# Two table transfers moved later in a spectral filter stage, with its written order of steps re-sorted

## The chip, the core and the metric

The kernel runs on one core of a Trainium2 chip. The core has a matrix engine (TensorE, PE in the profile) that multiplies a 128-row weight tile by a streamed operand into PSUM, a vector engine (DVE), a scalar engine (ACT), a general-purpose engine (GpSimd, POOL) and a sync engine (SP) that mostly issues transfers. Each works through its own list of instructions in order, and they wait for each other through semaphores. 16 DMA engines carry the transfers, whoever issues them. The metric is the device time of one launch in microseconds: 997.96 us, the median of three runs of the kernel before (997.35 to 1001.58).

## What is computed

A block of four layers on x of shape 2048 x 640 (sequence by channels), each with a residual:

```python
x = x + A(layernorm(x)); x = x + B(layernorm(x)); x = x + A(layernorm(x)); x = x + B(layernorm(x))

def A(x):   # spectral filter: the filter stage of the title lies in here
    X = rfft2(x, axes=(-2, -1)) * (w_r + 1j * w_i)      # 2048 x 321 complex weights
    return irfft2(X, s=(2048, 640))

def B(x):   # token MLP with a GELU; w1 is 2048 x 1728, w2 is 1728 x 2048
    u = gelu(einsum("bsd,sf->bdf", x, w1) + b1)
    return transpose(einsum("bdf,fs->bds", u, w2) + b2)
```

## The kernel before

The Fourier transforms are done as matrix products with small tables, in float16 high and low parts so that a product of two split operands takes three matmuls. A layer A has a first part (`a0_...`: normalise, fold, transform along the long part of the sequence), the **filter stage** (`a1`) and a last part (`a2`: the inverse transform and the residual). `a1` runs twice in a launch, once per layer A; the first time (`first=True`) it also carries side work for later stages, hung in by the function `also`.

The filter stage takes 16 groups of frequencies, g = 0 to 15. Each group goes through steps that the code names by letters, the number behind them being the group:

- `d` (PE): products of the folded rows with the table tD, and with `stk`, a small stacked tile that SP brings for two groups at a time (three buffers; the load for groups n and n+1 waits until d of n-6 and n-5 have read theirs).
- `ph` (ACT) and `pl` (DVE): the high and low float16 parts of that result.
- `sA`, `sB` (PE): the two halves of the next small transform, with table tS2.
- `tb`, `ta` (DVE, `term`): the result times the filter weights `w[g]`. A weight tile of 321 KB is loaded by SP (`wload`); there are three buffers, and the load for group n is written down as soon as `ta` and `tb` of n-3 are.
- `sa`, `sb` (POOL, `suma` and `sumb`): the difference and sum that make the complex product. In the trace both write tile `ta`.
- `xh` (ACT), `xl` (POOL), `uh`, `ul` (ACT, `twice`): split into high and low parts, and a copied strip.
- `i` (PE, `is2mm`), `Yh` (ACT), `Yl` (DVE): first half of the inverse transform, and its split into the tile Y.

Four PSUM tiles (`slots`) hold what `d`, `sA`/`sB` and `i` write; the `@k` behind a step says which. A step may only write its slot when the readers of the last content are done: for instance `d10@1` writes the slot that `ta6` and `tb6` read.

The order of all steps is written out by hand in the string `STEPS`; the loop at the end of `a1` goes through it, and since everything in it is recorded with a mark that keeps program order (`self.pin`), each engine gets its own steps in the order of that string. The order between steps of different engines in the string has no meaning by itself, but three things hang on it: the place at which SP's loads of `w` and `stk` are written down (the code that follows `do(op)` in the loop), the place of the side work (`also`), and, in the kernel before, which ACT step after an `sA` is chosen for a dependency: `sB` of a group is made to follow one ACT step that itself follows `sA` (list `waiting`, function `acted`).

Two tables for `a2` are loaded during the filter stage from the POOL queue: tDi (966 KB) and the first of four parts of tIM (512 KB, tile `tIM0`). In the kernel before, both are issued behind `sb3`:

```python
if g == 3:
    with self.after(ins):
        nc.gpsimd.dma_start(self.tDi, A["tDi"])
        nc.gpsimd.dma_start(self.tIM0, A["tIM"][:, 0:4])
```

`a2` starts with products of Y and tDi (`id_mm`), and uses `tIM0` one step later (`is1_mm`). Nearly every instruction bears line 69 in the profile, that of the helper that records it (line 70 in the changed file, whose `STEPS` is one line longer), so tiles are the way to tell instructions apart. The loads keep their own lines: `w` L506, `stk` L494 and L496, tDi L654, tIM0 L655.

Of the kernel before, what the change touches and what calls it, by code (L numbers as in the profile page):

```python
# [24 lines left out]
FIRST = 2  # L25
WARM = 11
STEPS = '''
    d1@1 sA0@2 ph1 pl1 sB0 d2@0 sA1@1 ph2 tb0 d3@3 ph3 sB1 ta0 sa0 pl2 sb0 xh0 xl0 sA2@0 tb1 uh0 pl3 d4@2 ta1 sa1 sb1
    sB2 ph4 ta2 sA3@3 d5@1 ul0 pl4 tb2 sB3 sb2 ph5 pl5 sA4@2 xh1 sa2 d6@0 d7@1 ta3 ph6 tb3 sB4 pl6 tb4 xl1 uh1 ph7
    sA5@3 xh2 i0@0 sb3 sB5 pl7 sa3 ta4 ul1 Yh0 Yl0 tb5 sA6@1 xl2 xh3 ta5 sb4 d8@2 ph8 d9@0 sa4 xl3 xh4 sB6 uh3 ul3 sa5  # L30
    pl8 tb6 sA7@3 uh2 sb5 i1@2 ph9 sB7 Yh1 xl4 ta6 pl9 d10@1 xh5 sb6 xl5 sA8@0 sa6 Yl1 ul2 ta7 ph10 i3@2 tb7 sB8 Yh3
    pl10 sA9@3 i2@1 ta8 uh4 sa7 xh6 ul5 tb8 sB9 Yl3 d11@0 ul4 sb7 Yh2 Yl2 xh7 xl6 uh6 sb8 sa8 uh5 sA10@2 tb9 ph11 xl7
    ta9 pl11 d12@1 xh8 sB10 sa9 ph12 sb9 i4@3 Yh4 i5@0 ta10 tb10 pl12 xh9 Yh5 xl8 d13@2 Yl4 sb10 ph13 sA11@1 ul6 Yl5
    uh8 pl13 sA12@3 sB11 sa10 ul7 xl9 xh10 xl10 sB12 ta11 tb11 ta12 sA13@2 d14@0 ph14 ul8 sa11 i6@1 sb11 ul9 Yh6 uh7
    sB13 tb12 pl14 Yl6 d15@3 xh11 sa12 uh9 sA14@0 tb13 sb12 ph15 xl11 i7@1 sB14 ta13 pl15 uh10 i8@2 ul10 uh11 xh12
    sa13 Yh7 sb13 i9@3 ul11 xh13 uh13 tb14 ta14 xl12 Yl7 sa14 uh12 Yh9 sA15@0 Yh8 sb14 Yl9 xh14 xl13 i10@1 sB15 i11@3
    Yh10 ul13 Yl8 xl14 i13@2 Yh11 uh14 tb15a ta15a ul14 ul12 sb15a Yh13 tb15b sa15a ta15b Yl10 Yl11 i14@0 Yl13 xh15a
    sb15b i12@1 sa15b xl15a xh15b uh15 xl15b i15a@2 Yh14 Yh12 Yl14 Yl12 ul15 Yh15a i15b@3 Yh15b Yl15a Yl15b
'''
SEQ = [t + 7 * i for t in (6, 0, 1, 2, 3, 4, 5) for i in range(2)]  # L40
EPS = 1e-5
# [35 lines left out]
class Layers:  # L77
# [367 lines left out]
    def a1(self, first):  # L445
        nc, A = self.nc, self.A
# [90 lines left out]
        def xhi(g, c, x):  # L537

            return T.activation(xs[g % NX][0][:, :, c], x, AF.Copy)
# [6 lines left out]
        def twice(g, i):  # L546

            q = xs[g % NX][i]
            return T.activation(q[:, :, NL:], q[:, :, 257:320], AF.Copy)
# [61 lines left out]
        w = {g: wload(g) for g in range(3)}  # L611
        pp, ps2, pv = {}, {}, {}
        slots = [self.big() for _ in range(4)]
        dst, half, waiting = {}, {}, []
        tt = collections.defaultdict(dict)
        part = {"": every, "a": slice(0, 256), "b": slice(256, NL)}
        ltile = {"": slice(0, 3), "a": slice(0, 2), "b": slice(2, 3)}
# [7 lines left out]
            T.activation(b, a, AF.Copy, scale=sc)  # L625
            V.scalar_tensor_tensor(c, a, sc, b, op0=ALU.mult, op1=ALU.subtract)

        def acted(ins):

            for g in waiting:  # L630
                follow(ins, half[g])
                half[g] = ins
            waiting.clear()

        def do(op):

            name, g, c, dve, k = re.fullmatch(r"([a-zABY]+)(\d+)([ab]?)(!?)(?:@(\d))?", op).groups()
            g, W, ps = int(g), V if dve else G, slots[int(k or 0)]
            pair = lambda: (tt[g][0], tt[g][1])
            if name == "d":  # L640
                dst[g] = psplit(dstage(g, ps))
            elif name == "ph":
                acted(next(dst[g]))
            elif name == "pl":
                pp[g] = next(dst.pop(g))
            elif name in ("ta", "tb"):
                term(g, name == "tb", part[c])
            elif name == "sa":
                suma(pair(), part[c], W)
            elif name == "sb":  # L650
                ins = sumb(pair(), part[c], W)
                if g == 3:
                    with self.after(ins):
                        nc.gpsimd.dma_start(self.tDi, A["tDi"])  # L654
                        nc.gpsimd.dma_start(self.tIM0, A["tIM"][:, 0:4])  # L655
            elif name == "xh":
                acted(xhi(g, part[c], tt[g][0][:, :, part[c]]))
            elif name == "xl":
                xlo(g, part[c], tt[g][0][:, :, part[c]], W)
            elif name in ("uh", "ul"):  # L660
                acted(twice(g, name == "ul"))
            elif name == "sA":
                ps2[g] = ps
                half[g] = s2half(g, ps, pp[g], 0)[1]
                waiting.append(g)
            elif name == "sB":
                follow(s2half(g, ps2[g], pp.pop(g), 1)[0], half.pop(g))
            elif name == "i":
                pv[g, c] = ps
                for lt in range(3)[ltile[c]]:  # L670
                    is2mm(ps, g, lt)
            elif name == "Yh":
                acted(yhi(g, pv[g, c], ltile[c]))
            elif name == "Yl":
                ylo(g, pv[g, c], ltile[c])

# [37 lines left out]
        for op in STEPS.split():  # L714
            do(op)
            if first:
                also(op)
            ended.add(op.split("@")[0])
            if wn < NG and {f"ta{wn - 3}", f"tb{wn - 3}"} <= ended:
                w[wn] = wload(wn)  # L720
                wn += 1
            k = sn - NSTK * NC
            if sn < NG and (k < G0 or {f"d{k}", f"d{k + 1}"} <= ended):
                stack(sn)
                sn += NC
# [1298 lines left out]
```

## Time and profile before

| | |
|---|---|
| median of 3 runs | 997.96 us (997.35, 997.96, 1001.58) |
| the profiled execution: its time, its span | 999.61 us, 997.8 us |
| PE busy | 949.3 us (95%) |
| DVE busy | 774.9 us (78%) |
| ACT busy | 575.1 us (58%) |
| POOL busy | 302.1 us (30%) |
| first filter stage, first `d` step after the start to the first product with tDi | about 62.8 to 124.6 us |
| second filter stage, likewise | about 556.7 to 621.3 us |

The span is the time from the first to the last instruction of the profiled execution, and the execution's own time is 1.8 us longer. Busy shares are averages over stages that have different limits; the two filter stages are the places in which PE is not busy all the time, and they are read apart below. A timeline row gives start, duration, engine, line, operation, tiles written and read, how many instructions of that kind follow each other, and in brackets the idle time of the engine before it and who ended it.

### The profile page before, as it was taken

To read this page: it belongs to the slowest core of one execution; us is meant where nothing else is said; L and a number is where in the kernel's file an instruction comes from. 1 tells how busy PE (TensorE), PEld (TensorE's weight loads), DVE (VectorE), ACT (ScalarE), POOL (GpSimd) and SP (SyncE) were. 2 spreads that over 40 slices of the span, in tenths; PEclk is the share of its full clock that TensorE was granted. 3 is DMA by queue.
4 is the path that set the end of the run, shared out by engine and by line. 5 is a ranking of instruction groups with operands and counts; after the bars stand their busy time and mean duration, and the time that the engine had idled before them with its cause. 6 is when DMAs were issued, how large, how long until landed. Compare 5 with 4: busy or idle time off the path is not lost.

```text
span 997.8 us, 22816 instructions
## 1 busy us (share of the span) xinstructions
PE 949.3 (95%) x9126; PEld 703.5 (71%) x9126; DVE 774.9 (78%) x1488; ACT 575.1 (58%) x888; POOL 302.1 (30%) x512
## 2 busy tenths in 40 slices
PE   3879999999999999999999888999999999999998
PEld 2767777677776777777777666776777777677776
DVE  7979989988677884666666779789955666998885
ACT  4857859698656565555544457684644445454431
POOL 6939857322112102222222388583000000000000
PEclk9589999999999999999999999999999999999999
DMA  7856357657667655464431564574555447655411
GB/s 231 279 176 205 98 196 240 221 211 271 216 231 238 207 161 201 127 215 127 129 107 51 174 190 130 166 235 167 169 169 159 138 143 258 218 173 196 146 48 51
DMA packets 67454, 176.30 MB, mean 177 GB/s; under 512 B 8122, under 2 KB 15444, under 8 KB 67348
## 3 DMA queue, kind: packets, MB, share of 16 engines
q1 hardware_dynamic: 59380, 146.39, 46.2%
q0 software_dynamic: 7968, 28.46, 7.6%
q8 instruction: 71, 1.16, 0.5%
q14 instruction: 35, 0.29, 0.1%
HBM read 127.24 MB, written 47.58 MB: 175 GB/s over the span
## 4 chain that ended last, share of the span: by engine, by line
PE 61%; DVE 14%; issue 10%; DMA 5%; ACT 5%; POOL 4%; SPq 0%; POOLq 0%; DVEq 0%; ACTq 0%
PE ps L69 61%; DVE st L69 2%; DVE f L69 2%; DVE xt L69 1%; DMA w1S<-sp 1%; DVE s1l L69 1%; DMA raw<-w2z 1%; DVE hl L69 1%; DMA xt<-x 1%; POOL xt L69 1%; DVE Yl L69 1%; DVE wl L69 1%; DMA w<-w 1%; POOL w1A L935 1%; DVE S L69 1%
## 5 line engine op out<-in xcount | busy, mean ns | idle before, releaser
L69 PEld LDWEIGHTS <-wh 128*128 128x128 f16 x2602 | 251.5, 98 | 101.0 <-issue 2.4
L69 PEld LDWEIGHTS <-wl 128*128 128x128 f16 x1610 | 157.4, 98 | 63.2 <-DVE wl L69 1.3
L69 PE MATMUL ps<-ul,wh 128*128 128x320 f16 x448 | 133.0, 299 | 0.0
L69 PE MATMUL ps<-uh,wl 128*128 128x320 f16 x448 | 133.1, 299 | 0.0
L69 PE MATMUL ps<-uh,wh 128*128 128x320 f16 x416 | 124.3, 299 | 0.0
L69 PE MATMUL ps<-hl,wh 128*128 128x320 f16 x496 | 102.2, 299 | 0.8 <-DVE hl L69 0.8
L69 PEld LDWEIGHTS <-wo 128*128 128x128 f16 x756 | 73.9, 98 | 29.4 <-DVE wo L69 0.8
L69 DVE SCALAR_TENSOR_TENSOR wl<-raw,s,wh 128x896 f16<-128x896 f32 (+2 forms) x63 | 73.8, 1175 | 23.7 <-ACT wh L69 21.7
L69 POOL TENSOR_TENSOR r<-v,mh 128x1 f32<-128x1 f32 x64 | 37.3, 583 | 158.4 <-DVE nm L69 148.8
L69 ACT ACTIVATE junk<-raw 128x896 bf16<-128x896 f32 (+1 forms) x60 | 59.5, 992 | 32.0 <-DMA raw<-w 28.8
L69 PE MATMUL ps<-tDi,Yh 128*128 128x322 f16 x320 | 71.3, 300 | 0.4 <-ACT Yh L69 0.3
L69 ACT ACTIVATE wh<-raw,s 128x896 f16<-128x896 f32 (+2 forms) x66 | 66.5, 1032 | 5.5 <-DVE s L69 4.9
L69 DVE TENSOR_TENSOR f<-eo 128x256 f32<-128x256 f32 (+1 forms) x124 | 39.0, 367 | 37.8 <-POOL eo L69 37.0
L69 POOL TENSOR_TENSOR xt<-xt,ec 128x320 f32<-128x320 f32 x64 | 53.2, 853 | 32.7 <-DVE xt L69 32.6
L69 ACT ACTIVATE z<-xt,nb,r 128x640 f32<-128x640 f32 x31 | 28.5, 919 | 54.2 <-POOL z L69 43.1
L69 PE MATMUL ps<-u,wo 128*128 128x320 f16 x420 | 59.0, 299 | 0.5 <-DVE wo L69 0.5
L69 DVE BATCH_NORM_STATS2 st<-xt 128x6 f32<-128x320 f32 x126 | 55.2, 479 | 5.3 <-DMA xt<-x 4.7
L69 PE MATMUL ps<-hha,wh 128*128 128x320 f16 x288 | 58.1, 299 | 0.9 <-DVE wh L69 0.9
L69 PE MATMUL ps<-tM,f 128*128 128x128 f32 x160 | 37.6, 402 | 21.7 <-DVE f L69 21.6
L69 POOL TENSOR_TENSOR eo<-z 128x320 f32<-128x320 f32 x60 | 52.2, 891 | 17.2 <-ACT z L69 15.2
L69 PE MATMUL ps<-tDi,Yl 128*128 128x322 f16 x192 | 55.7, 299 | 1.4 <-DVE Yl L69 1.4
L69 PE MATMUL ps<-hha,wl 128*128 128x320 f16 x256 | 53.4, 299 | 1.0 <-DVE wl L69 1.0
(254 smaller groups left out, 2335.5 us busy)
## 6 DMA issues: line engine op xcount, KB each, us to landing
xt<-x SPq DMA_DIRECT2D x79, 320.0 KB
raw<-w SPq DMA_DIRECT2D x32, 512.0 KB
w<-w SPq DMA_DIRECT2D x48, 321.0 KB
x<-xt SPq DMA_DIRECT2D x47, 320.0 KB
raw<-w SPq DMA_DIRECT2D x32, 448.0 KB
raw<-w2z SPq DMA_DIRECT2D x32, 448.0 KB
w1S<-sp POOLq DMA_DIRECT2D x20, 512.0 KB, 3.9
out<-xt SPq DMA_DIRECT2D x15, 320.0 KB
```

The lines of the kernel that those rows point to most:

```text
L69: i = f(*a, **k)
L935: (self.nc.sync if k else self.nc.gpsimd).dma_start(st[:, i], w[i][:, c * q:c * q + q])
```

## The change

It does four things.

1. The steps in `STEPS` are written in another order. On each single engine the order of the steps stays what it was; only how the four lists are interleaved in the string differs.
2. The choice of the ACT step that an `sB` follows is no longer derived from the place in the string but written down with the step (`ph1&0` means: this step is the one between `sA0` and `sB0`). The pairs are those of before.
3. tDi is loaded in two halves (its high and its low part), behind `sb7` and `sb9`, and the first part of tIM behind `sb11`; before, both were loaded whole behind `sb3`.
4. Since loads and side work are written down where the string puts them, a few of these move: in both filter stages SP's load of `w` for group 3 comes ahead of the `stk` load for groups 8 and 9 instead of behind it, and in the first filter stage five side instructions on ACT stand one place earlier or later.

```diff
 STEPS = '''
-    d1@1 sA0@2 ph1 pl1 sB0 d2@0 sA1@1 ph2 tb0 d3@3 ph3 sB1 ta0 sa0 pl2 sb0 xh0 xl0 sA2@0 tb1 uh0 pl3 d4@2 ta1 sa1 sb1
+    d1@1 sA0@2 ph1&0 pl1 sB0 d2@0 tb0 ta0 sA1@1 d3@3 ph2&1 sa0 sb0 pl2 sB1 ph3 sA2@0 tb1 xh0 d4@2 uh0&2 pl3 xl0 ta1
...
-        def acted(ins):
+        def acted(ins, gs):
 
-            for g in waiting:
+            for g in map(int, gs.split(",") if gs else ()):
                 follow(ins, half[g])
                 half[g] = ins
-            waiting.clear()
...
-                if g == 3:
+                if g in (7, 9, 11):
                     with self.after(ins):
-                        nc.gpsimd.dma_start(self.tDi, A["tDi"])
-                        nc.gpsimd.dma_start(self.tIM0, A["tIM"][:, 0:4])
+                        if g < 11:
+                            nc.gpsimd.dma_start(self.tDi[:, g // 9], A["tDi"][:, g // 9])
+                        else:
+                            nc.gpsimd.dma_start(self.tIM0, A["tIM"][:, 0:4])
```

**POOL in the second filter stage**, around the loads of tDi and tIM; before (`xl` ... is the step `xl1`, the row behind it `sb3`, then the two loads, `sa3`, `xl2`):

```order
L69 TENSOR_TENSOR xl_1063_8366<-ta_8699,xh_1063_8365 128x2x321
L69 TENSOR_TENSOR ta_8879<-tb_8884,ta_8879 128x321
L654 DMA tDi_8359<-tDi 128x3864
L655 DMA tIM_8358<-tIM 128x1024
L69 TENSOR_TENSOR ta_8879<-ta_8879,tb_8884 128x321
L69 TENSOR_TENSOR xl_1063_8368<-ta_8720,xh_1063_8367 128x2x321
```

and in the changed kernel (`sa7`, `sb7`, the first half, `xl6`, `sb8`, `sa8`, `xl7`, `sa9`, `sb9`, the second half, `xl8`):

```order
L70 TENSOR_TENSOR ta_9216<-ta_9216,tb_9259 128x321
L70 TENSOR_TENSOR ta_9216<-tb_9259,ta_9216 128x321
L655 DMA tDi_8360<-tDi 128x1932
L70 TENSOR_TENSOR xl_1063_8367<-ta_9149,xh_1063_8366 128x2x321
L70 TENSOR_TENSOR ta_9291<-tb_9333,ta_9291 128x321
L70 TENSOR_TENSOR ta_9291<-ta_9291,tb_9333 128x321
L70 TENSOR_TENSOR xl_1063_8369<-ta_9216,xh_1063_8368 128x2x321
L70 TENSOR_TENSOR ta_9444<-ta_9444,tb_9405 128x321
L70 TENSOR_TENSOR ta_9444<-tb_9405,ta_9444 128x321
L655 DMA tDi_8360<-tDi 128x1932
L70 TENSOR_TENSOR xl_1063_8371<-ta_9291,xh_1063_8370 128x2x321
```

The two issues behind `sb3` are gone; a half-size issue stands between `sb7` and `xl6`, another between `sb9` and `xl8`, and the load of tIM likewise between `sb11` and `sa12`. POOL's other instructions keep their order.

**SP in the second filter stage**, around the load of `w` for group 3 (`w_8644` before, `w_8577` now); the `stk` tile for groups 8 and 9 is `stk_8621` before and `stk_8623` now, that for groups 6 and 7 `stk_8519`. Before:

```order
L494 DMA stk_8621<-rest_12_1063_8376 32x4x256
L496 DMA stk_8621<-rest_12_1063_8376 1x256
L506 DMA w_8644<-w 128x642
L506 DMA w_8701<-w 128x642
L895 DMA raw_10415<-w 128x1024
```

and now:

```order
L495 DMA stk_8519<-rest_12_1063_8377 32x4x256
L497 DMA stk_8519<-rest_12_1063_8377 1x256
L507 DMA w_8577<-w 128x642
L495 DMA stk_8623<-rest_12_1063_8376 32x4x256
L497 DMA stk_8623<-rest_12_1063_8376 1x256
```

The load of `w` for group 3 has moved ahead of the five issues for `stk` of groups 8 and 9; behind them the load for group 4 and that of a weight tile of layer B (`raw`) follow as before.

**ACT in the first filter stage**, around the side work on `raw` (the sums of squares, `junk`). Before (`ul1`, `Yh0`, `junk`, `xh3`, `ph8`, `xh4`, `uh3`, `ul3`, `junk`, `uh2`):

```order
L69 ACTIVATE xl_219_881<-xl_219_881 128x2x63
L69 ACTIVATE Yh_871<-ps_908 128x2x96x4
L69 ACTIVATE junk,sq_1527<-raw_1418 128x1024
L69 ACTIVATE xh_219_884<-ta_1411 128x2x321
L69 ACTIVATE ph_1580<-ps_910 128x2x321
L69 ACTIVATE xh_219_886<-ta_1515 128x2x321
L69 ACTIVATE xh_219_884<-xh_219_884 128x2x63
L69 ACTIVATE xl_219_885<-xl_219_885 128x2x63
L69 ACTIVATE junk,sq_1527<-raw_1420 128x1024
L69 ACTIVATE xh_219_882<-xh_219_882 128x2x63
```

and now:

```order
L70 ACTIVATE xl_219_881<-xl_219_881 128x2x63
L70 ACTIVATE Yh_871<-ps_908 128x2x96x4
L70 ACTIVATE xh_219_884<-ta_1372 128x2x321
L70 ACTIVATE junk,sq_1572<-raw_1419 128x1024
L70 ACTIVATE ph_1613<-ps_910 128x2x321
L70 ACTIVATE xh_219_886<-ta_1515 128x2x321
L70 ACTIVATE xh_219_884<-xh_219_884 128x2x63
L70 ACTIVATE junk,sq_1572<-raw_1421 128x1024
L70 ACTIVATE xl_219_885<-xl_219_885 128x2x63
L70 ACTIVATE xh_219_882<-xh_219_882 128x2x63
```

The first `junk` now stands behind `xh3`, the second ahead of `ul3`; three more side instructions (one on b1, two splits of a weight tile) change places with a neighbour in the same way. DVE's list and PE's are the same in both kernels.

36 lines of the change are left out of this document (18 added, 18 removed).

## The prediction

> **What bounds the kernel now.** I read the stages of the trace first, then the chain of work that ended last inside the second filter stage, then the timelines there. The stretches are the first filter stage, what lies between, the second filter stage, and the rest; behind the stretch and its length come busy times of PE, weight loads, DVE, ACT and POOL with counts, the granted clock, the DMA share and GB/s:
>
> ```profile
> 62.80:124.60 61.80, 56.08 (x1484) 45.01 (x1480) 55.13 (x101) 45.17 (x93) 48.77 (x62) 0.99 0.51 152
> 124.60:556.70 432.10, 426.46 (x3278) 311.22 (x3280) 322.12 (x733) 264.04 (x372) 115.92 (x218) 1.00 0.56 184
> 556.70:621.30 64.60, 57.16 (x1487) 46.57 (x1484) 52.34 (x82) 40.65 (x83) 49.01 (x62) 0.96 0.55 167
> 621.30:997.80 376.50, 369.68 (x2696) 267.12 (x2696) 292.48 (x429) 182.65 (x245) 43.58 (x70) 1.00 0.50 163
> ```
>
> Between and behind the filter stages PE is busy 98 to 99% of the time, so a microsecond gained in a filter stage reaches the end. The second one is the longer by 2.8 us although it carries no side work, and its clock is lower. The chain of waits there (start, length, what) says why:
>
> ```profile
> 576.11 0.80 DVE ta L69
> 576.92 7.30 DMA w<-w
> 584.34 0.20 DVE tb L69
> 585.14 0.89 DVE ta L69
> 586.07 14.04 PE ps L69 x344
> ```
>
> One transfer of filter weights takes 7.30 us, and nothing else in the stage has a piece of that kind. The timeline around it:
>
> ```profile
> 574.76 0.57 POOL L654 DMA_DIRECT2D tDi<-tDi  x1
> 575.32 0.56 POOL L655 DMA_DIRECT2D tIM<-tIM  x1
> 576.92 3.00 SPq L506 DMA_DIRECT2D w<-w  x3
> 579.48 0.82 DVE L69 SCALAR_TENSOR_TENSOR pl<-ps,ph 128x642 f16<-128x642 f32 x1
> 584.34 0.89 DVE L69 SCALAR_TENSOR_TENSOR tb<-ps,sx,w 128x642 f32<-128x642 f32 x1 [4.04 <-DMA w<-w]
> 586.07 0.48 PE L69 MATMUL ps<-tD,s1h 128*64 128x160 f16 x4 [4.01 <-DVE ta L69]
> 590.37 0.83 DVE L69 SCALAR_TENSOR_TENSOR pl<-ps,ph 128x642 f16<-128x642 f32 x1 [1.11 <-ACT ph L69]
> ```
>
> By its place in DVE's list the late `tb` is `tb6`, and the load is that of `w` for group 6. It is issued 2.2 us behind tDi and 1.6 us behind tIM. DVE stands for 4.04 us; behind it stand `ta6`, and PE with `d10`, whose PSUM slot `ta6` reads: 4.01 us. Four more stretches (columns as above) show the transfers at their limit during that wait, what PE's clock does behind it, and who is busy from then on:
>
> ```profile
> 576.50:584.50 8.00, 5.38 (x144) 4.42 (x137) 3.90 (x7) 4.98 (x10) 7.06 (x8) 1.00 1.01 339
> 586.05:589.30 3.25, 3.23 (x44) 2.43 (x43) 3.21 (x5) 0.00 (x0) 2.83 (x3) 0.50 0.37 106
> 591.20:611.70 20.50, 20.35 (x564) 16.12 (x556) 20.49 (x32) 16.49 (x38) 18.59 (x20) 1.00 0.52 159
> 84.00:89.00 5.00, 4.32 (x118) 3.46 (x113) 4.51 (x8) 4.08 (x11) 5.00 (x7) 1.00 1.07 363
> ```
>
> In the 8 us around the wait the DMA engines are full and move 2.7 MB (339 GB/s). Of this, tDi and tIM are 1.5 MB (966 and 512 KB). After the wait PE runs at a granted clock of 0.50 for 3.25 us. From 591 to 612 PE and DVE are both busy without a gap and POOL nearly so. The last row is from the first stage: there the engines are full too, but no DVE row waits for `w`.
>
> **The change, part by part.**
>
> *The stall at `tb6` (second stage).* With tDi and tIM gone from here, 1.5 of the 2.7 MB are gone. What is left for `w` of group 6 to wait for is its own queue. The nearest row for its landing is the load of group 3, issued with the load of group 4 and the 512 KB `raw` behind it:
>
> ```profile
> 568.26 0.99 SPq L506 DMA_DIRECT2D w<-w  x2
> 572.17 0.89 DVE L69 SCALAR_TENSOR_TENSOR ta<-ps,sx,w 128x642 f32<-128x642 f32 x1 [0.21 <-DMA w<-w]
> ```
>
> It took 3.91 us from issue to use. `tb6` can start when DVE is through with `pl8`, at 584.34 - 4.04 = 580.30, 3.38 us after the issue. So the load comes 0.53 us late if it takes as long as that row, and not at all if it is quicker. The issue itself should come sooner: the load of group 3 moves ahead of five `stk` issues on SP (they wait for `d3`, the load only for `ta0` and `tb0`), so 0.33 MB leave the crowded stretch from 568 on, about 1 us at the rate above. That also removes the 0.21 us of `ta3`. I take 0.2 us late, with 0 and 0.53 as bounds.
>
> Gone with the wait is the slow clock: 3.25 us at 0.50 instead of 1.00 is 1.6 us for PE, so PE could gain 4.01 + 1.6 = 5.6 us. DVE follows directly: 4.04 and the 1.11 us that `pl10` waited for the slow `d10`, 5.15 us. DVE then has 20.49 us of work in 20.50 us, so it is the narrower one, and I take its figure: 5.15 - 0.2 = 4.95 us.
>
> *The new places of the three issues (second stage).* Each issue held POOL for 0.56 to 0.57 us; a half-size one is not in the trace, and I take the same. Behind `sb3` POOL gets 1.13 us back. The one behind `sb7` falls into a wait:
>
> ```profile
> 592.61 1.42 POOL L69 TENSOR_TENSOR xl<-ta,xh 128x642 f16<-128x642 f32 x1 [1.75 <-ACT xh L69]
> 597.48 0.74 POOL L69 TENSOR_TENSOR ta<-tb,ta 128x321 f32<-128x321 f32 x1
> ```
>
> That row is `xl6`, which has 1.75 us to spare. The second half stands behind `sb9` (the row at 597.48), tIM behind `sb11`, both where POOL works without a break: 1.13 us later for `xl8`, `sb12` and what follows. Queued behind them are `ul` and `xh` on ACT and then `i` on PE. If all of it reaches PE, 1.13 us are lost; POOL's idle share of that stretch (20.50 - 18.59 = 1.91 us) would absorb it. Nearer to that row, I take 0.4 us.
>
> *The moved transfers.* They now meet later loads of `w`. Those have more room than group 6 had:
>
> ```profile
> 594.63 0.87 DVE L69 SCALAR_TENSOR_TENSOR tb<-ps,sx,w 128x642 f32<-128x642 f32 x1
> 595.42 0.88 DVE L69 SCALAR_TENSOR_TENSOR ta<-ps,sx,w 128x642 f32<-128x642 f32 x1
> 603.45 0.87 DVE L69 SCALAR_TENSOR_TENSOR ta<-ps,sx,w 128x642 f32<-128x642 f32 x1
> 621.27 0.45 PE L69 MATMUL ps<-tDi,Yh 128*128 128x322 f16 x2
> ```
>
> The load for group 12 may go when `tb9` and `ta9` are done (596.30) and is first used by `ta12` at 603.45: 7.15 us, the tightest of groups 9 to 13. A half of tDi is 0.49 MB, 1.5 us at 339 GB/s; 3.91 + 1.5 = 5.4 us still fits. The cover is 1.7 us; without it each load costs what its lateness is. tDi is first used at 621.27, 24 us behind `sb9`; whole, it landed in 5.9 us:
>
> ```profile
> tIM<-tIM POOLq DMA_DIRECT2D x2, 512.0 KB, 5.5
> tDi<-tDi POOLq DMA_DIRECT2D x1, 966.0 KB, 5.9
> ```
>
> So both tables are in time, and the moved transfers cost nothing there.
>
> *The first filter stage.* No `w` is late here, so only POOL's and ACT's lists matter.
>
> ```profile
> 82.54 0.78 POOL L69 TENSOR_TENSOR ta<-ta,tb 128x321 f32<-128x321 f32 x1
> 87.70 1.04 ACT L69 ACTIVATE junk<-raw 128x1024 bf16<-128x1024 f32 x1
> 88.74 0.29 ACT L69 ACTIVATE xh<-xh 128x126 f16<-128x126 f16 x1
> 89.08 0.33 PE L69 MATMUL ps<-ph,tS 64*64 64x321 f16 x4 [0.76 <-ACT xh L69]
> ```
>
> `sB7` waits 0.76 us for `uh2` on ACT, and that came late behind a `junk` of 1.04 us and POOL's chain. `sa3` (82.54) moves up by 1.13 us, and the `junk` no longer waits for `ul3`. So 0 to 0.76 us are won; later the same issues as above cost 0 to 1.13 us in a stretch where POOL has less idle time to share out (POOL is 5.00 of 5.00 us busy from 84 to 89), of which the 1.13 us won at `sb3` pay a part. I take the middle of 0 and 0.76, a gain of 0.4 us. SP's swap makes the `stk` load of groups 8 and 9, issued from 71.66 on, wait for `w` of group 3, which goes as soon as `ta0` and `tb0` are done, here at 72.10; its first reader `d8` starts at 83.54, so that is hidden:
>
> ```profile
> 71.22 0.88 DVE L69 SCALAR_TENSOR_TENSOR ta<-ps,sx,w 128x642 f32<-128x642 f32 x1
> 71.66 0.30 SPq L494 DMA_DIRECT2D stk<-rest  x1
> 83.54 0.33 PE L69 MATMUL ps<-tD,s1h 128*64 128x160 f16 x4
> ```
>
> *Explicit pairs* for `sB` cost nothing: they are those of before.
>
> **The sum.** 4.95 - 0.4 + 0.4 = 4.95 us. Against the profiled execution's 999.61 us (span 997.8 and 1.8 us around it) that gives 994.7 us. That execution was 1.65 us above the median of the runs, 997.96 us, and I take the gain off the median: **993.0 us**.
>
> **The rivals.**
>
> *The queues share evenly.* If SP's and POOL's transfers took turns, group 6 would have had half of the engines all along, and taking POOL's away would only halve the data part of its 7.30 us. With a fixed part between 0 and the 3.91 us of the row above, it would then land after 3.65 to 5.6 us: 0.3 to 2.2 us late. For it speaks that three `w` loads and one `stk` load stood in SP's queue as well. Against it, tDi and tIM landed by 580.8 (574.76 + 5.9, 575.32 + 5.5) and group 6 not before 584.2, so POOL's seem to have had most. At 2.2 us late the gain is 5.15 - 2.2 - 0.4 + 0.4 = 2.95 us: 995.0 us. The Trainium skill has this rule ("DMA: Bandwidth & Descriptors", section "SWDGE vs HWDGE vs iDMA"): each DMA engine goes round-robin between its internal queues, and those fed by GpSimd and those fed by the sync engine are different ones. The landing times just named fit it only if a turn of tDi is much longer than a turn of `w`.
>
> *POOL becomes the bound.* The three issues (1.7 us) stand where POOL is 91 to 100% busy. Before, it could wait for the late DVE in between, here at `sb6`:
>
> ```profile
> 586.10 0.75 POOL L69 TENSOR_TENSOR ta<-tb,ta 128x321 f32<-128x321 f32 x1 [2.54 <-DVE ta L69]
> ```
>
> If DVE and PE could come 5 us sooner but POOL could not, what remains is POOL's own waits, the 2.54 us here and the 1.75 us at `xl6`, less 1.7: 2.6 us. With the first stage losing 1.1 us the time is 996.5 us. Against it: the 1.13 us at `sb3` come back.
>
> *Slower.* A moved transfer meets a load of `w` and DVE stops as it did at `tb6`, in a stretch where it has no spare time. It decides from 7.15 us of landing time on; a wait of 4 us needs 11.2 us. Each such wait is worth 4.0 + 1.6 us with the clock behind it: 997.96 - 4.95 + 5.6 = 998.6 us if it comes in one stage, 1004.2 us in both. A DMA share of 0.52 in that stretch, where the wait at `tb6` had 1.01, speaks against it.
>
> *It doesn't do what it says.* The order on each engine is unchanged, so the sorting alone is worth nothing; if `w` of group 6 were late for SP's own traffic alone, the time stays at 997 to 999 us. The full engines with 1.5 of 2.7 MB from POOL speak against that.
>
> **How the numbers follow.** Forecast 0.74, with a range of its own of 991 to 995; even sharing 0.09; POOL as the bound 0.06; slower 0.07; nothing 0.04. About what a measurement of this kernel can tell from no change is 0.5%, 5.0 us, so the bound for faster is 992.97 us, and the forecast stands on it. Its best end is PE's 5.6 us with 0.76 us from the first stage and nothing lost to POOL, 991.6 us; its worst 0.53 us late, 1.13 us lost to POOL and no gain in the first stage, 994.5 us; half a microsecond on each side is for the runs' own spread. I put half of the forecast, 0.37, on faster; the other half with sharing, POOL and nothing, 0.56, on the same; 0.07 on slower. The range for 8 in 10 is 990.6 to 997.5: it takes in sharing and POOL, and leaves out slower, most of nothing and a little below.
>
> **What would show it.** In the changed profile the second filter stage should have no PE idle piece of several microseconds in front of `d10`, `tb6` should wait for `w` at most 0.5 us, and the granted clock of that stage should be near 1.00; its length should fall from 64.6 to about 60. In the first stage the wait of `sB7` should shrink. If PE instead waits in the second half for `xl`, `ul` or `xh`, the POOL term was too small; if `tb6` still waits 1 us or more, the sharing rival is right; a wait of 1 us or more at `tb9` to `tb13` with `w` as the releaser would make the forecast wrong on the slower side.

## The result, and the profile after

The changed kernel takes **991.58 us** (median of 5 runs, 990.41 to 991.67) against 997.96 us of the kernel before (5 runs, 997.35 to 1001.58): a ratio of 0.9926, with a 95% interval of 0.9911 to 0.9941. On a second chip, later, it took 991.93 us (5 runs, 990.50 to 992.84) beside 997.63 us: 0.9947 (0.9934 to 0.9960). The forecast was 993.0 us and put most of its weight on no measurable change; what came is a gain of about 6 us, beyond the 0.5% that the prediction had set as the bound (on the second chip just beyond it: 0.53%, with an interval that begins at 0.40%).

The same four stretches of the profile after, cut as far ahead of the first `sA0` of a stage, and as near the first product with tDi, as before (stretch, length, busy time of PE, weight loads, DVE, ACT and POOL, granted clock, DMA share, GB/s):

```profile
61.15:121.95 60.80, 55.67 (x1482) 44.47 (x1478) 54.92 (x101) 45.98 (x95) 49.58 (x63) 1.00 0.55 160
121.95:552.95 431.00, 425.42 (x3260) 310.00 (x3260) 320.95 (x732) 264.34 (x373) 116.01 (x218) 1.00 0.55 184
552.95:613.40 60.45, 55.87 (x1501) 45.23 (x1502) 53.60 (x84) 40.99 (x83) 49.34 (x63) 1.00 0.61 184
613.40:989.80 376.40, 369.66 (x2696) 267.10 (x2696) 292.55 (x428) 182.58 (x245) 43.58 (x70) 1.00 0.50 163
```

The profiled execution took 991.63 us, with a span of 989.8 us: 8.0 us less than the profiled one before. Of these, 4.15 us are in the second filter stage (64.60 to 60.45) and 1.0 us in the first (61.80 to 60.80). 1.1 us lie between the stages and 1.65 us ahead of the first one, where the change moves nothing. Those are dealt with under the first experiment.

DVE's rows in the second stage after the change, at the place of the late load (in brackets the idle time before a row), with SP's loads of `w` and POOL's three issues:

```profile
570.20 0.35 SPq L507 DMA_DIRECT2D w<-w  x1
574.25 3.16 SPq L507 DMA_DIRECT2D w<-w  x3
575.38 0.89 DVE L70 SCALAR_TENSOR_TENSOR tb<-ps,sx,w 128x642 f32<-128x642 f32 x1 [0.41 <-DMA w<-w]
577.72 0.89 DVE L70 SCALAR_TENSOR_TENSOR tb<-ps,sx,w 128x642 f32<-128x642 f32 x1
584.19 0.57 POOL L655 DMA_DIRECT2D tDi<-tDi  x1
590.34 0.56 POOL L655 DMA_DIRECT2D tDi<-tDi  x1
597.84 0.54 POOL L657 DMA_DIRECT2D tIM<-tIM  x1
```

`tb6` (577.72) starts without a wait; its load of `w`, issued at 574.25, was there within 3.47 us, where it took 7.30 us before. What is left is 0.41 us at `tb5`, the step one group earlier. Half a table costs POOL 0.57 and 0.56 us, as much as a whole one. The stretch of 8 us around the place, and the 20.5 us from the first issue on:

```profile
572.10:580.10 8.00, 7.75 (x212) 6.39 (x208) 7.59 (x12) 6.31 (x13) 7.79 (x9) 1.00 0.67 192
584.10:604.60 20.50, 20.08 (x551) 15.73 (x545) 19.73 (x31) 16.27 (x37) 20.45 (x24) 1.00 0.73 234
```

The DMA share in the crowded 8 us has gone from 1.01 to 0.67, and PE's busy time there from 5.38 to 7.75 us. The bytes are now in the later stretch (0.73 instead of about 0.5), where PE is still busy 20.08 of 20.50 us and POOL has no idle time left.

In the first stage the waits of PE, from `d4` to the first product with tDi, were before (us in total, times, longest):

```profile
PE ps L69 <- DVE Yl L69: 2.1, 4, 0.8
PE ps L69 <- ACT xh L69: 0.8, 1, 0.8
PE ps L69 <- ACT xl L69: 0.4, 1, 0.4
PE ps L69 <- DVE ta L69: 0.3, 1, 0.3
PE ps L69 <- ACT Yh L69: 0.3, 1, 0.3
```

and after:

```profile
PE ps L70 <- DVE Yl L70: 2.3, 4, 1.0
PE ps L70 <- DVE ta L70: 0.4, 1, 0.4
PE ps L70 <- ACT Yh L70: 0.2, 1, 0.2
```

Two waits for ACT are gone, that of `sB7` (`xh`, 0.8) and one for `xl` (0.4) that the prediction did not speak of; those for `Yl` and `ta` are longer by 0.2 and 0.1 us.

### The profile page after: what moved, and what is told of

It is laid out like the page before. It is cut to its first block, busy times and chain, and to the rows that moved or that the text cites. A ratio compares the mean times of both kernels' runs of the same rounds, so it can differ in the third digit from the quotient of the medians.

```text
span 989.8 us, 22823 instructions
## 1 busy us (share of the span) xinstructions
PE 946.2 (96%) x9126; PEld 700.2 (71%) x9126; DVE 774.9 (78%) x1488; ACT 575.6 (58%) x888; POOL 302.9 (31%) x514
## 4 chain that ended last, share of the span: by engine, by line
PE 62%; DVE 10%; issue 10%; DMA 7%; POOL 5%; ACT 5%; SPq 0%; POOLq 0%; ACTq 0%; DVEq 0%
PE ps L70 62%; DMA xt<-x 2%; DMA w<-w 2%; DVE xt L70 1%; DVE hl L70 1%; DVE st L70 1%; POOL xt L70 1%; DMA raw<-w2z 1%; POOL w1A L936 1%; DMA w1S<-sp 1%; DVE f L70 1%; DVE s1l L70 1%; DVE S L70 1%; DVE wl L70 1%; POOL eo L70 1%
```

## The experiments

The theory: the 7.30 us of the one load of `w`, behind tDi and tIM, are nearly all of it in the second stage; POOL's 1.13 us and the moved side steps make the 1 us in the first. The rivals: that the re-sorted list and SP's swap do part of it; that POOL's new issue places take part of it away; that what delays the load is not the bytes.

| run | median, runs | kernel before beside it | ratio (95%) | wait of `tb6` in the trace |
|---|---|---|---|---|
| loads alone | 991.41, 8 | 997.54 | 0.9944 (0.9925-0.9963) | none (`tb5` 0.31) |
| order alone | 997.21, 12 | 997.54 | 1.0000 (0.9984-1.0016) | 3.00 |
| loads, second stage only | 992.77, 12 | 997.54 | 0.9956 (0.9939-0.9973) | none |
| before, again | 998.87, 12 | 997.54 | 1.0016 (1.0000-1.0033) | 4.39 |
| changed, again | 991.93, 5 | 997.63 | 0.9947 (0.9934-0.9960) | 0.39 |
| tIM back | 992.55, 11 | 997.63 | 0.9948 (0.9930-0.9966) | 1.27 |
| six issues | 994.00, 12 | 997.63 | 0.9969 (0.9958-0.9980) | 2.40 (see there) |
| raw later | 991.75, 7 | 997.63 | 0.9947 (0.9929-0.9965) | none |
| tDi back on POOL | 994.84, 12 | 997.61 | 0.9966 (0.9946-0.9986) | 3.28 |
| tDi on SP, ahead of `w` | 996.11, 12 | 997.61 | 0.9976 (0.9954-0.9998) | 1.84 |
| tDi on SP, last | 993.33, 12 | 997.61 | 0.9955 (0.9936-0.9973) | none |
| both of the last ideas | 993.58, 12 | 997.61 | 0.9955 (0.9935-0.9975) | none |

Times are in us. Rows with the same figure for the kernel before ran on one chip.

### The kernel before, again

No edit.

> The kernel before, unchanged, for a second trace of it and for the scatter of one kernel against itself: 0 within 0.5 us. The wait of about 4 us at tb6 and the granted clock of 0.5 behind it should be there again. Open is the granted clock at the start of the second filter stage (0.50 at 556 to 558 us in the trace of before, 1.00 in that of the change): if it belongs to the kernel it is low here too, if it is chance it is not, and then up to 1.4 us of the 8.0 us between the two profiled spans is not the change's.

The kernel against itself gives 1.0016, and its 12 runs lie between 996.1 and 1001.8 us: single executions of one kernel differ by several microseconds. The trace shows one source. The granted clock (next to last but one number of a row) at the start of the second stage, in the first trace of before and in this one:

```profile
555.60:559.00 3.40, 3.40 (x56) 3.40 (x58) 1.23 (x2) 0.24 (x1) 1.71 (x3) 0.54 0.94 302
```

```profile
560.20:563.70 3.50, 3.50 (x56) 2.69 (x53) 0.92 (x2) 0.71 (x1) 1.45 (x2) 0.53 0.32 88
```

PE ran at half clock for about 3.4 us both times, the first time ahead of `sA0`, the second time behind `d2`. The first trace of before also had such a stretch at the start of the first stage, twice as long; the second one had none there:

```profile
57.00:63.80 6.80, 5.62 (x56) 4.98 (x58) 2.83 (x6) 4.14 (x10) 1.46 (x3) 0.50 0.78 263
```

In the other traces they came, or not, around the starts of either filter stage, with the loads at the old places and at the new. Two examples with loads moved: the loads alone, at the start of the first stage, and tDi on SP ahead of `w` (see below), at the start of the second, again of the double length:

```profile
67.80:71.20 3.40, 3.40 (x53) 2.59 (x50) 2.77 (x6) 0.71 (x1) 1.28 (x2) 0.50 0.30 80
```

```profile
562.60:569.40 6.80, 6.59 (x94) 5.03 (x94) 2.08 (x4) 2.04 (x3) 1.45 (x2) 0.52 0.46 131
```

So they are not the change's, and 3.4 us at half speed are worth up to 1.7 us where PE has work throughout. The trace of the change happened to have none from the first stage on. The stretches from 57 and from 555.6 us in the trace of before both lie ahead of an `sA0`; they are large enough for the 2.75 us outside the filter stages, and the reason why the spans of two single traces must not be subtracted. The Trainium skill ("TensorE: Matmul & The Clock Gate", section "Part 1: The HAM clock gate (the 'warmup' mystery)") says that the gate watches windows of about 3.4 us that run freely, without regard to the program. The lengths of these stretches (3.4 and 6.8 us) and their coming and going agree with that.

To compare the stages without those stretches, I take each from `d4`, behind the start, to the first product with tDi. Before, and after, `d4` and the product in the first stage:

```profile
73.42 0.33 PE L69 MATMUL ps<-tD,s1h 128*64 128x160 f16 x4
124.65 0.31 PE L69 MATMUL ps<-tDi,Yh 128*128 128x322 f16 x1 [0.27 <-ACT Yh L69]
```

```profile
71.77 0.33 PE L70 MATMUL ps<-tD,s1h 128*64 128x160 f16 x4
122.01 0.45 PE L70 MATMUL ps<-tDi,Yh 128*128 128x322 f16 x2 [0.22 <-ACT Yh L70]
```

and in the second stage, before (the product is at 621.27, in the prediction) and after:

```profile
566.81 0.33 PE L69 MATMUL ps<-tD,s1h 128*64 128x160 f16 x4
```

```profile
564.07 0.33 PE L70 MATMUL ps<-tD,s1h 128*64 128x160 f16 x4
613.34 0.45 PE L70 MATMUL ps<-tDi,Yh 128*128 128x322 f16 x2
```

Read the same way, the traces give (us):

| | first stage | second stage |
|---|---|---|
| before; before again | 51.23; 51.24 | 54.46; 54.27 |
| changed; changed again | 50.24; 50.25 | 49.27; 50.03 |
| loads alone | 50.39 | 49.62 |
| order alone | 50.51 | 52.67 |
| loads, second stage only | 51.55 | 48.85 |
| tIM back | 50.21 | 49.16 |
| six issues | 51.26 | 52.67 |
| raw later | 50.20 | 48.95 |
| tDi back on POOL | 50.20 | 53.73 |
| tDi on SP, last | 51.12 | 49.59 |

By the means of the first two lines the change is worth 1.0 us in the first stage and 54.37 - 49.65 = 4.7 us in the second, 5.7 us together.

One wait in the second stage blurs this. It stands before the same matmul in most traces, 7.9 us ahead of the product with tDi, and no engine or load of the profile ends it ("issue"). Before, before again, changed, changed again:

```profile
613.37 0.21 PE L69 MATMUL ps<-tI,xl 64*128 64x128 f16 x1 [1.08 <-issue]
```

```profile
611.46 0.21 PE L69 MATMUL ps<-tI,xl 64*128 64x128 f16 x1 [0.78 <-issue]
```

```profile
605.44 0.21 PE L70 MATMUL ps<-tI,xl 64*128 64x128 f16 x1 [1.03 <-issue]
```

```profile
606.63 0.21 PE L70 MATMUL ps<-tI,xl 64*128 64x128 f16 x1 [1.80 <-issue]
```

Its length is no property of the kernel: 1.03 and 1.80 us in two traces of one file, none with tIM back. Without it the second stage takes 53.38 and 53.49 us before and 48.24 and 48.23 us after, so what the change does there is 5.2 us, and each pair agrees to about 0.1 us. The same figure is 48.15 us for the loads alone (two such waits, 1.47 us), 48.11 for the loads in the second stage only, 48.11 for raw later, and 52.11 for the order alone. A transfer of 0.02 MB in the queue that the page calls `instruction` lies some 2 to 3 us ahead of the wait's end in the traces of before, the change and the change again, but also ahead of that place with tIM back, where PE did not wait. What ends the wait is not shown, nor whether the moved loads lengthen it: it was 0.56 to 1.08 us in three traces with both loads at the old place in that stage, and 0.74 to 1.80 us in five with the three loads at the new places.

### The loads alone, and the order alone

Loads alone: the file before, with only this edit.

```diff
-                if g == 3:
+                if g in (7, 9, 11):
                     with self.after(ins):
-                        nc.gpsimd.dma_start(self.tDi, A["tDi"])
-                        nc.gpsimd.dma_start(self.tIM0, A["tIM"][:, 0:4])
+                        if g < 11:
+                            nc.gpsimd.dma_start(self.tDi[:, g // 9], A["tDi"][:, g // 9])
+                        else:
+                            nc.gpsimd.dma_start(self.tIM0, A["tIM"][:, 0:4])
```

> The kernel before with only the three loads at their new places (tDi halves behind sb7 and sb9, tIM behind sb11, in both filter stages); the step list and the pairs are those of before, so SP issues w of group 3 behind the stk load of groups 8 and 9 again. Theory A (the time of the change is that of the late w of group 6 behind tDi and tIM, and of POOL's 1.1 us at sb3): 6.0 to 6.6 us below the kernel before, within 0.5 us of the changed kernel; tb6 of the second stage does not wait for w. Theory B (SP's swap matters as well, since it brings w of group 3 and with it 4 and 5 earlier): 1 us or more above the changed kernel, with tb4, tb5 or tb6 waiting 1 us for w. My prediction had the loads at 5.0 us and SP's swap at no more than 0.2 us.

Order alone: the changed file, with that edit taken back.

> The changed kernel with tDi (whole) and tIM back behind sb3: what is left of the change is the sorted list with its written pairs, SP's swap and five ACT steps of the first stage that change places. Theory A: within 0.5 us of the kernel before, and the wait of about 4 us at tb6 is there again. Theory B: 1 us or more below the kernel before, because w of group 3 leaves SP earlier and w of group 6 lands earlier; the wait at tb6 is then 3 us or less.

The loads alone are 6.1 us below the kernel before, and 991.41 us stands beside 991.58 and 991.93 us of the change. The order alone is at 1.0000. With the loads alone only a small wait for `w` is left, at `tb5`; with the order alone the large one at `tb6` is there (with the piece of the chain of waits that ends in it):

```profile
575.04 0.89 DVE L69 SCALAR_TENSOR_TENSOR tb<-ps,sx,w 128x642 f32<-128x642 f32 x1 [0.31 <-DMA w<-w]
```

```profile
580.63 0.89 DVE L70 SCALAR_TENSOR_TENSOR tb<-ps,sx,w 128x642 f32<-128x642 f32 x1 [3.00 <-DMA w<-w]
574.52 5.99 DMA w<-w
```

Theory A holds: the places of the loads make the gain. The trace of the order alone looks 1.7 us better in the second stage than that of before (3.00 instead of 4.04 us of wait), but this execution, 995.37 us, was the fastest of its 12; by the ratio of all runs SP's swap is worth nothing that can be measured, with an interval of 1.6 us to each side.

In the first stage each half brings most of the 1.0 us by itself: 0.85 us with the loads alone, 0.7 us with the order alone. The remaining waits of PE tell them apart. With the loads alone the one for `xh` is gone and that for `xl` is left; with the order alone it is the other way round, and 0.2 of the 0.8 us for `xh` are left:

```profile
PE ps L69 <- ACT xl L69: 0.4, 1, 0.4
```

```profile
PE ps L70 <- ACT xh L70: 0.2, 1, 0.2
```

So both parts shorten `sB7`'s wait, which can be won only once, and the order takes the `xl` wait in addition. In that stage it moves SP's swap and the side steps on ACT; that it is the side steps is likely, since the wait is for ACT, but no run parts the two.

### The loads moved in the second stage only, and the change again

```diff
-                if g == 3:
+                if first and g == 3:
                     ...
+                if not first and g in (7, 9, 11):
+                    ...
```

> The kernel before with the three loads at their new places in the second filter stage alone. Theory A: the second stage is the whole of it but for the 1.0 us that the first stage was shorter in the trace of the change: 5.0 to 5.6 us below the kernel before. If the two stages' gains do not add up to the 6.4 us of the change (a first stage worth 2 us or more, or worth nothing), the 1.0 us read off the one trace of each was wrong. My prediction gave the second stage 4.55 us and the first 0.4 us.

4.8 us below the kernel before, and 1.4 us above the loads alone in both stages; its first stage is as long as before (51.55 us, of which 0.46 us are a wait that no engine ends), its second as short as in the change. The intervals overlap (0.9956 and 0.9944), so the 1 us of the first stage rests on the traces, which agree; the times only do not contradict it.

> The changed kernel, unchanged, for a second trace of it and for more runs beside those of the kernel before on one chip. The three loads alone came out at 0.9944 of the kernel before, the change at 0.9926. If both are the same thing, this run lies between them, 5.5 to 6.5 us below; if the sorted list adds something of its own (the first stage was 1.0 us shorter in the trace of the change), 6.5 to 7.4 us below. tb6 of the second stage should not wait; the granted clock should not fall in that stage, unless it falls by chance in front of d2.

5.7 us by the medians, 5.3 us by the ratio, which lies beside that of the loads alone. The sorted list adds nothing that shows. The trace repeats the first one: no wait at the old size, 0.39 us at `tb6`.

### How much of the tables stands in front

tIM back: the changed file with `g in (3, 7, 9)`, tIM at 3. tDi back on POOL: `g in (3, 11)`, tDi whole at 3. tDi on SP: tDi whole, the last thing that SP issues ahead of `w` of group 6, which is behind the last transfer of `stack(12)`; tIM stays at 11.

```diff
+            if g == 12:
+                with self.after(ins):
+                    nc.sync.dma_start(self.tDi, A["tDi"])
```

> The changed kernel with the 512 KB of tIM back behind sb3 and the halves of tDi left behind sb7 and sb9. Theory A (what stands in front of w of group 6 is data: it lands when the tables that were issued before it are through): with 1.48 MB there tb6 waited 3.0 us (the run with both tables back); 1.48 MB take 4.4 us at the 339 GB/s of that stretch, so the load has 1.4 us to spare without them; 0.51 MB take 1.5 us, and tb6 waits 0.1 us, 0.5 at most. The time is then within 1 us of the changed kernel. Theory B (a table load in front costs the load of w a fixed time, whatever its size): tb6 waits 1.5 us or more, and the time is 3 us or more above the changed kernel with the slow clock behind the wait.

> The changed kernel with tDi, whole (966 KB), back behind sb3 on POOL's queue and tIM left behind sb11. tb6 waited not at all with nothing there, 1.27 us with the 512 KB of tIM, 3.00 us with both (1.48 MB). Theory A (bytes in front; a line through the two points gives 1.8 us per MB and 0.4 us at nothing): tb6 waits about 2.1 us, 1.6 to 2.6. Theory B (turns between the queues, so that no table holds the load of w for longer than its own 0.32 MB take at half the rate, about 1 us, whatever the table's size): about the 1.27 us of tIM, 1.0 to 1.5. The time is 1.5 to 4 us above the changed kernel by A, the upper end with a slow clock behind the wait, and up to 1.5 us by B.

> As the run with tDi whole in front of w of group 6, but issued by SP, the last thing ahead of that load in SP's own queue; tIM stays behind sb11. Theory A (POOL's queue is served before SP's or as if it stood ahead in one queue): tb6 waits as long as with tDi on POOL's queue, or longer by the time by which SP issues it later. Theory B (the queues take turns, and only within one queue does the load wait for all of a table): tb6 waits clearly longer here, 966 KB at 339 GB/s being 2.8 us against the 1 us of a turn-taking queue: 2.5 to 3.5 us.

The row of `tb6` and the piece of the chain in front of it (the time from the issue of `w` to its landing), for tIM back, tDi back on POOL, and tDi on SP:

```profile
577.10 0.89 DVE L70 SCALAR_TENSOR_TENSOR tb<-ps,sx,w 128x642 f32<-128x642 f32 x1 [1.27 <-DMA w<-w]
572.79 4.18 DMA w<-w
```

```profile
580.97 0.89 DVE L70 SCALAR_TENSOR_TENSOR tb<-ps,sx,w 128x642 f32<-128x642 f32 x1 [3.28 <-DMA w<-w]
574.16 6.69 DMA w<-w
```

```profile
584.49 0.89 DVE L70 SCALAR_TENSOR_TENSOR tb<-ps,sx,w 128x642 f32<-128x642 f32 x1 [1.84 <-DMA w<-w]
579.23 5.14 DMA w<-w
```

With 0, 0.51, 0.97 and 1.48 MB in front of it `w` landed after at most 3.47 us (the change), 4.18, 6.69 and 5.99 to 7.30 us. More data in front makes it later up to tDi's size, and tIM on top adds nothing clear; tDi is the transfer that mattered most. The row with nothing in front has one exception, the trace of six issues below. Both theories missed here: 1.27 us lies above the 0.1 to 0.5 us that a queue by bytes would give and below the 1.5 us of a fixed price, and 3.28 us above the 2.1 us of the line. That the queues take turns is not borne out in the form in which it was put: by that theory the wait does not grow with the table and is longer with tDi in SP's own queue. It grew from 1.27 to 3.28 us, and with tDi right ahead in SP's queue the load landed sooner (5.14 us) than with tDi on POOL's (6.69 us). These are single traces, and the last two differ in more than the queue: in the 2.2 us up to the issue of `w` the DMA share was 0.91 with tDi on POOL and 0.50 with tDi on SP. So turns are not excluded, and why the load came later behind POOL's transfer is open. The medians of the last two, 994.84 and 996.11 us, are in the other order. The trace of tDi on SP shows one place where time went: the 6.8 us at half clock from 562.6 us on, ahead of `d4`; from `d4` on its two stages take 50.61 and 50.23 us. Whether the place of tDi brings that stretch on, one trace can't show.

The row of tIM back shows one more thing: a wait of 1.27 us at `tb6` made PE wait 1.13 us, but no slow clock followed, and the median is within 1 us of the change.

### What POOL's issues cost

Six issues: each of the three loads cut in two at its place.

```diff
+                        for c in (slice(0, 2), slice(2, 4)):
                             if g < 11:
-                            nc.gpsimd.dma_start(self.tDi[:, g // 9], A["tDi"][:, g // 9])
+                                c = slice(c.start, min(c.stop, 3))
+                                nc.gpsimd.dma_start(self.tDi[:, g // 9, c], A["tDi"][:, g // 9, c])
                             else:
-                            nc.gpsimd.dma_start(self.tIM0, A["tIM"][:, 0:4])
+                                nc.gpsimd.dma_start(self.tIM0[:, c], A["tIM"][:, c])
```

> The changed kernel with each of the three loads cut in two: six issues on POOL at the same three places, three more than before, 1.7 us more of POOL per stage at 0.56 us each, with the same bytes. Theory A (POOL's idle time and its waits for ACT take them up): no more than 0.5 us above the changed kernel. Theory B (what an issue costs POOL in this stretch reaches PE, the term that I set at 0.4 us of 1.13): at 0.35 of their length 0.6 us per stage, 1.2 us in both; if all of it reaches PE, 3.4 us, with PE waiting for ta, xl or ul in the second half of both stages.

2.1 us above the change (994.00 against 991.93), between "covered" and "all of it". The trace shows where, first in the first stage, which is 1.0 us longer. Up to 112 us PE keeps step with the changed kernel; then ACT waits for POOL and PE for ACT:

```profile
112.45 0.74 ACT L70 ACTIVATE xh<-ta 128x642 f16<-128x642 f32 x1 [0.99 <-POOL ta L70]
```

```profile
115.18 0.33 PE L70 MATMUL ps<-ph,tS 64*64 64x321 f16 x4 [0.94 <-ACT Yh L70]
```

The second stage has the same wait at its tail, behind an `xh` that POOL held up by 1.09 us; the trace of the change has none of this kind there:

```profile
610.16 0.33 PE L70 MATMUL ps<-ph,tS 64*64 64x321 f16 x4 [0.98 <-ACT Yh L70]
```

So POOL's lateness does not cost where the issues stand but at the tail of either stage, about 1 us each. The second stage lost more at `tb6`, which waited 2.40 us though no table was in front. The trace names POOL's `xl` as the releaser:

```profile
579.42 1.42 POOL L70 TENSOR_TENSOR xl<-ta,xh 128x642 f16<-128x642 f32 x1
580.88 0.89 DVE L70 SCALAR_TENSOR_TENSOR tb<-ps,sx,w 128x642 f32<-128x642 f32 x1 [2.40 <-POOL xl L70]
```

By their places in the lists the same `xl` starts behind the start of `tb6` in the trace of the change (578.56 against 577.72), so `tb6` does not need it. The load of `w` is the likelier cause; issued at 575.68, it would then have taken up to 5.2 us with no table ahead of it. So the 3.47 us are not what the load always takes, and what delayed it here is open.

tDi on SP, last: the three issues cut to one instead, with tDi whole behind the load in `wload(15)`.

```diff
+            if g == NG - 1:
+                with self.after(ins):
+                    nc.sync.dma_start(self.tDi, A["tDi"])
```

> The changed kernel with tDi whole, issued by SP behind the load of w of group 15 in both stages, so that POOL has one issue left (tIM behind sb11) instead of three. With three issues more on POOL the time rose by 2.1 us, and the first stage by 1.0 us in the trace: 0.6 of their length. Theory A (an issue of POOL in the second half reaches PE at that share, so my term for POOL was too small as a price): two issues less are 1.13 us less of POOL, 0.7 us per stage, and the time is 1.2 to 1.6 us below the changed kernel. Theory B (the rise came from w of group 6, which was late in that trace, not from POOL): within 0.5 us of the changed kernel. Against both: tDi now lands 16 us before its first use instead of 20, and in front of five loads of x.

The time does not follow Theory A: with two issues less it is 993.33 us, not 990.4 us. The second stage (49.59 us) is as in the change; the first is 0.9 us longer, with a wait of PE that no engine ends, before the same kind of matmul as the one above:

```profile
121.98 0.21 PE L70 MATMUL ps<-tI,xl 64*128 64x128 f16 x1 [1.28 <-issue]
```

The waits of that kind, 1.5 us in this first stage, hide a gain: without them it takes 49.57 us, 0.7 us less than in the change, and PE waits 2.0 us for other engines instead of 2.9 us. So in the times fewer issues bring nothing, though the trace shows some of their price in the first stage; six cost 1 us a stage in the trace and 2.1 us by the times. Where the wait comes from, and whether tDi's new place lengthens it, is open.

### What else stands in front of `w`

raw later: SP issues the 512 KB of `raw` (second stage) behind `w` of group 7 instead of behind that of group 4. The first lines stand in `wload(g)`.

```diff
-            nc.sync.dma_start(w, A["w"][g])
+            ins = nc.sync.dma_start(w, A["w"][g])
+            if g == 7:
+                self.late = ins
...
-                self.wload(1)
+                with self.after(*([] if first else [self.late])):
+                    self.wload(1)
```

> The changed kernel with the 512 KB of raw, which SP issues between w of groups 4 and 5 in the second stage, issued behind w of group 7 instead. In the trace of the change tb5 waited 0.41 us for w of group 5, which took 5.05 us from its issue. Theory A (the same mechanism on a small scale, here within one queue: data issued earlier comes first): that wait is gone, w of group 5 lands in less than 4 us, and the time is 0.3 to 0.5 us below the changed kernel, less than these runs can tell. Theory B (w of group 5 is late for another reason, such as stk's many small pieces): the wait stays at 0.3 to 0.5 us. A price that either leaves out: raw meets later loads of w, whose first reader may then wait.

As Theory A had it: no DVE row of that stage waits for `w`, the stage is at 48.95 us, and the time, 991.75 us, cannot be told from that of the change (991.93 us).

The two together, tDi on SP last and raw later:

> The run with tDi on SP behind w of group 15, and raw of the second stage behind w of group 7 as in the run in which no w was late. If the two are worth 1.4 us and 0.4 us and do not touch each other, 1.8 us below the changed kernel, which would be 989.9 to 990.2 us beside its 991.6 to 991.9 us; if POOL's price is not real, 0.4 us below at most.

993.58 us: nothing is won over the change. With tDi at the same place the "issue" waits of the first stage are only 0.2 us in this trace, so they are not the whole reason why the two versions with tDi last on SP take longer. No version that I ran beats the change measurably.

## Why the prediction was right or wrong

*What bounds the kernel* held: what was gained in the filter stages reached the end.

*The stall at `tb6`* held as a mechanism. The loads alone make the gain, and the wait comes back with the tables. The size was a little too small: without the "issue" wait the second stage gained 5.2 us, which is DVE's 5.15 us whole and not PE's 5.6 us, so taking DVE's figure was right. The 0.2 us taken off for a late load do not show. `tb6` waited 0.39 us in one trace (the change again) and not at all in those of the change, the loads alone and the loads in the second stage only; in the trace of six issues the load seems to have been far later than the bound of 0.53 us. One reason given was wrong: the earlier issue of `w` of group 3 did not matter, since the loads alone, without SP's swap, do as well. That the plain means give 4.7 us, close to the 4.95 - 0.4 = 4.55 us forecast, is luck as far as is known: the "issue" wait was 0.5 us longer in the two traces of the change.

*POOL's new issue places, -0.4 us*: this step failed too, in size. With 5.2 us won of 5.15 us nothing is left that POOL could have cost in the second stage. In the first stage two of PE's waits for ACT went, and no wait for POOL's sake came. The worry was not empty: three issues more cost about 1 us a stage, at its tail and not where the issues stand.

*The first stage, +0.4 us*: this is the step that failed by most. I took the middle of 0 and 0.76 us, "the middle" standing for an unknown loss on POOL. The traces give 1.0 us, above the upper bound. The bound counted only `sB7`'s wait. The change also took away the 0.4 us for `xl`, which stood in the same list of waits and was not priced; 0.3 us came back at `Yl` and `ta`.

*The moved transfers, SP's swap, the explicit pairs, each at nothing* held in the second stage: behind group 6 no DVE row waits for `w` in the trace of the change, and the order alone is at 1.0000. "The order on each engine is unchanged, so the sorting alone is worth nothing" did not hold in the first stage: ACT's side steps changed places, and the order alone shortened that stage by 0.7 us in its trace.

*The sum.* With 1.0 instead of 0.4 us in the first stage and 5.2 us instead of 4.55 us in the second it is 6.2 us, 991.8 us from the median used. Measured were 6.4 us on one chip and 5.7 us on the other; the "issue" wait (0 to 1.8 us) and the half-clock stretches (up to 1.7 us for each 3.4 us) are large enough for the differences.

*The chances.* The bound for "faster" stood on the forecast itself, so the small terms, 1.25 us too low together, decided on which side the result came out. Most of the weight of "the same" came from giving half of the forecast to it, and from the rivals. Of these, even sharing left a wait of 0.3 to 2.2 us at `tb6`, which the traces of the change and of the loads alone do not show but for 0.39 us in one; POOL as the bound fell for three issues; slower and no effect did not come.

## What to carry to other kernels

A load that a tight step waits for is delayed by large transfers issued shortly ahead of it on another queue: move these to where the next load has slack, and price the stall once, on the engine that becomes the narrower one. When a change moves small steps as well, list every wait of the bound engine in that stage and say which of them go, instead of pricing the largest and taking the middle. Compare stages between two steps of the program, over two traces of each kernel, before a span is subtracted from a span, and look for a wait whose length changes between two traces of one kernel.

## What was not expected of the hardware

- PE's granted clock fell to one half for 3.4 or 6.8 us, mostly around the starts of the filter stages, in some executions and not in others of the same kernel; 3.4 us of it cost up to 1.7 us, large enough for a part of the scatter of 996.1 to 1001.8 us of one kernel.
- The mean granted clock of an execution did not tell its time (0.998 in the trace of six issues with a span of 993.7 us, 0.984 in that of the change with 989.8 us). In 11 of the 14 traces the clock was also at a half from about 20 to 50 us or longer, in the other three it was not, and the first `d` step came no sooner there (59.4 to 59.8 us, against 59.0 to 60.7 us). From 30 to 40 us DVE was busy 9.9 of 10 us in the trace of the change, at half clock, and in that of before again, at full clock.
- Inside a stage the clock fell behind PE waits of 4.0, 4.2, 3.25 and 2.8 us, and not behind waits of 2.4, 1.7 and 1.1 us. The Trainium skill (the page and section named above) says that the slow state comes after an idle window of about 3.4 us; here 2.8 us of waiting was enough in one trace.
- `w`, issued 0.45 us behind a 966 KB load in SP's own queue, landed after 5.14 us; issued 2.0 us behind the same load on POOL's queue, after 6.69 us. The Trainium skill ("DMA: Bandwidth & Descriptors", section "SWDGE vs HWDGE vs iDMA") says that a DMA engine takes turns between the queues that these two feed. Equal turns would make the second the shorter one, and these two traces do not show that; the DMA engines were busier ahead of the second.
- Cutting a POOL load in two costs a second issue of full length: 0.57 and 0.56 us for the halves of tDi, 0.57 us for the whole.
